# Chunk 2's first product in half-size products, keys-values and last numerators in one burst, and a preparation spread over two chunks

## The chip, the cores and the metric

The kernel runs on one core of a Trainium2 chip. The metric is the device time of one execution in microseconds, the median of three runs. One further execution was profiled; all rows quoted here come from it.

## The reference

Two steps follow each other: a linear attention with cosine weights, and a two-layer MLP with a swish whose slope is learned per hidden unit.

```
B, H, S, D = 8, 8, 576, 64
q_p, k_p = [relu(x)*cos_w, relu(x)*sin_w]          # 2*D features per head
kv  = einsum('bhsf,bhsd->bhfd', k_p, v)             # keys-values
z   = sum(k_p, axis=2)
num = einsum('bhsf,bhfd->bhsd', q_p, kv)            # numerators
den = einsum('bhsf,bhf->bhs', q_p, z) + 1e-6
x   = (num/den), laid out as [4608 tokens, 512]
h   = x @ w_in                                      # 512 -> 2048
g   = h / (1 + exp(-beta*h))
out = g @ w_out                                     # 2048 -> 512
```

## The kernel before

The attention is worked on batch by batch (8 batches of 576 tokens, or nine blocks of 64), the MLP chunk by chunk (nine chunks of 512 tokens, or eight blocks). Chunk c needs the last blocks of batch c-1 and the first ones of batch c. While chunk c goes through the MLP, the attention of batch c+1 and the preparation of later batches run beside it. All matmul operands are bf16, sums are in PSUM, which has eight banks (`ps`).

A batch passes through these steps. Its q, k and v are loaded on SP's queue (`load_raw`, one buffer each). `q_relu` writes `qb`; a transposing DMA on SP's queue (`q_turn_dma`, TQ) turns it into `qts`, of which there are two, one for even and one for odd batches; `q_tan` multiplies that by a tangent into the second half of the query features (`qs_of`), on GpSimd (POOL in the profile) or VectorE (DVE). `k_relu` writes `rk`. `v_scale` writes `vb`, the values times the cosine and times the sine, in nine steps each. `kv_mm` (L276) makes the keys-values from `rk` and `vb` with 72 matmuls of 64x64 tiles in two PSUM banks; `kv_take` (L286) copies them to `kv`. `num_mm` (L297) makes the numerators with 64x64 tiles, `num_all` a third of a batch (three of nine token groups, both head pairs, 48 matmuls). `x_part` divides (L308, L312, L319) into `xs` and turns it with a transposing DMA into the chunk's `xt` (L367).

A chunk's MLP has two halves, named h and o here. In full size, h is 16 groups of four 128x512 matmuls (`h_mm`, L386), each followed by the swish on ScalarE (ACT; `h_act`, L394). In half-size products (the scheme of Strassen and Winograd), a pair of groups takes seven products of halves instead of eight, each two matmuls of 256 columns (`h_pair`, L511), and sums before and after them: sums of weights (`wh_sum`, L443, once for all chunks), sums of x (`x_sum`, L455, four per chunk), and in PSUM a copy to a second bank on ACT (`seed`, L480), a copy to SBUF (`keep`, L484) and two additions on DVE (`add`, L487) per pair; the swish is `h_silu` (L420). The second product, o, is in half-size products from chunk 1 on: 2 x 7 products of eight matmuls with 256 columns (`o_fast`, L562, in chunk 1; `o_pair`, L620, from chunk 2 on), with sums of g on DVE (`g_sum`, L406, 16 per chunk). Chunks 0 to 2 make h in full size, chunks 3 to 8 in half size.

The scheduling is manual: every engine and every queue carries out its instructions in the order in which the program issues them, and waits where data or a buffer is not ready. Up to chunk 2's h the order is written as Python (the slots, `h_first`). From then on it is written out in `ORDERS`, one string of steps per chunk, which `chunk` issues from left to right:

- `h35` is product 5 of pair 3 of h; `1` and `c` name a PSUM bank behind them (`h110`, `h1c6`). `ox`, `oy` are o's two halves. `c` is the seed, `d`/`D` the keep on ACT/DVE, `e` and `f` the additions, `A`, `B` the swish of h, or the copies of o out of PSUM on ACT (`X`, `Y` on DVE).
- `s21` is g_sum of kind 2 for the second four groups of g, `W51` the weight sum of kind 1 for pair 5, `t1` an x_sum of the next chunk.
- `K00` and `K1` are keys-values for the two head pairs (bank 0 and the next), `kT` the copy to `kv`; `N12` numerators of third 1 in bank 2 and the next, `x1` their division and turn.
- `k`, `v`, `w`, `q`, `g`, `TQ`, `L` prepare and load later batches: k_relu on ACT, values times sine on ACT, times cosine on DVE, q_relu on DVE, tan on POOL, the turn of q, the loads.

Where `g` is issued, `q_tan` makes POOL wait for the DVE step that `chunk` remembers as `last`:

```
    def q_tan(b, jp, behind=None):
        got = tan_mul(nc.gpsimd, qs_of(b)[:, jp], qts[b % 2][:, jp], 0, NQ)
        after(got, behind, "GpSimd behind a copy")
```

Stores of o are issued on POOL's queue up to chunk 6 (`store`, L536).

Of the kernel before, what the change touches and what calls it, by code (L numbers as in the profile page):

```python
# [16 lines left out]
P = 128  # L17
# [5 lines left out]
def kernel(  # L23
# [175 lines left out]
    def k_relu(b, j0=0, j1=4, eng="dve", n0=0, n1=NQ):  # L199
        relu(rk.rearrange("q n j d -> q j n d")[:, j0:j1, n0:n1], raw_tile(b, "k")[:, j0:j1, n0:n1], eng)  # L200
# [48 lines left out]
    def qs_of(b):  # L249
        return wx["q"] if b > 3 and b % 2 == 0 else qs_first  # L250
# [15 lines left out]

    def kv_out(jp, bank):
        return ps[:, bank : bank + 2, jp * 2 * E : (jp + 1) * 2 * E]
# [12 lines left out]
    def kv_take(jps, bank, eng="dve"):  # L281
        a0, a1 = jps[0], jps[-1] + 1
        o = kv[:, :, a0:a1].rearrange("q g s c e -> q g (s c e)")
        a = ps[:, bank : bank + 2, a0 * 2 * E : a1 * 2 * E]
        if eng == "act":
            nc.scalar.copy(o, a)  # L286
        else:
            nc.vector.tensor_copy(o, a)

    def num_mm(b, n, jp, bank, slot):  # L290

        for cs in range(2):
            for jj in range(2):
                rows = slice(jj * HP, (jj + 1) * HP)
                for g in range(2):
                    cols = slice(g * HP, (g + 1) * HP)
                    nc.tensor.matmul(  # L297
                        ps[cols, bank + jj, slot * E : (slot + 1) * E],
                        lhsT=(qts[b % 2], qs_of(b))[cs][rows, jp, n, cols],
                        rhs=kv[rows, g, jp, cs, :],  # L300
                        start=(cs == 0), stop=(cs == 1))

    def x_rden(bank, slot, n0, n1, jps):

        w, m = len(jps), n1 - n0
        nv = ps[:, bank : bank + 2, slot * E : (slot + w * m) * E].rearrange("q j (i s e) -> q j i s e", s=w, e=E)
# [25 lines left out]
    def num_all(b, t, bank):  # L332
        for i in range(3):
            for jp in range(2):
                num_mm(b, 3 * t + i, jp, bank, 2 * i + jp)
# [37 lines left out]
    def h_bank(c, jt):  # L373
        if c < 2 and jt < 4:
            return ((3, 2, 5, 0), (6, 7, 4, 5))[c][jt]
        if c == 2 and jt in (10, 11):
            return jt - 8
        return ((6, 7, 4, 5) if c == 0 else (0, 1, 4, 5))[jt % 4]
# [43 lines left out]
    def wx_tiles():  # L422
# [8 lines left out]
            BF16)[:, 0 : 2 * NQ * P].rearrange("q (s n c) -> q s n c", s=2, n=NQ)  # L431
# [123 lines left out]
    def o_fast(c, pr, banks):  # L555

        b_ps, e_ps, a_ps = (ps[:, k_, 0:HM] for k_ in banks)
        tok = slice(pr * P, (pr + 1) * P)

        def prod(dst, left, right, start, stop):  # L560
            for i in range(JT // 2):
                nc.tensor.matmul(dst, lhsT=left(i), rhs=right[:, i], start=start and i == 0,  # L562
                                 stop=stop and i == JT // 2 - 1, skip_group_check=True)

        def g_part(r, hf):
            def at(i):
                jt = 2 * i + r
                return gs[c, jt // 4][:, jt % 4, hf * (TCH // 2) + pr * P : hf * (TCH // 2) + (pr + 1) * P]
            return at

        def s_part(t):
            return lambda i: t[:, i, tok]

        o1 = osb_pool.tile([P, DM], FP32, name="o_sb", tag="o_sb")
        o2 = osb_pool.tile([P, DM], FP32, name="o_sb", tag="o_sb")
        p1 = part.tile([P, HM], FP32, name="p1", tag="p1")
        p5 = part.tile([P, HM], FP32, name="p5", tag="p5")
        u = part.tile([P, HM], FP32, name="u", tag="u")

        def c4():  # L580
            nc.scalar.copy(o2[:, 0:HM], b_ps)

        def stored(key, op):
            def do():
                op()
                waits[key[0]].discard(key[1:])
                if not waits[key[0]]:
                    store(c, pr + (2 if key[0] == "2" else 0), o2 if key[0] == "2" else o1)
            return do

        waits = {"1": {"a2", "a3"}, "2": {"a7", "c4"}}
        add = dict(op=ALU.add)
        return {
            "1": lambda: prod(b_ps, g_part(0, 0), B11, True, False),
            "5": lambda: prod(e_ps, s_part(S1), T1, True, False),
            "6": lambda: prod(b_ps, s_part(S2), T2, False, False),
            "2": lambda: prod(a_ps, g_part(1, 0), B21, True, True),
            "7": lambda: prod(b_ps, s_part(S3), T3, False, False),
            "3": lambda: prod(e_ps, s_part(S4), B22, False, True),
            "4": lambda: prod(b_ps, g_part(1, 1), T4, False, True),  # L600
            "c1": lambda: nc.scalar.copy(p1, b_ps),
            "c5": lambda: nc.scalar.copy(p5, e_ps),
            "cu": lambda: nc.scalar.copy(u, b_ps),
            "c4": stored("2c4", c4),
            "a2": stored("1a2", lambda: nc.vector.tensor_tensor(o1[:, 0:HM], a_ps, p1, **add)),
            "a3": stored("1a3", lambda: nc.vector.tensor_tensor(o1[:, HM:DM], e_ps, u, **add)),
            "a7": stored("2a7", lambda: nc.vector.tensor_tensor(o2[:, HM:DM], b_ps, p5, **add)),
        }


# [107 lines left out]
    kv_take((0,), 6, eng="act")  # L718
# [14 lines left out]
    kv_take((1,), 6, eng="act")  # L733
# [56 lines left out]
    def second():  # L790
# [18 lines left out]
        22: lambda: (kv_mm(1, 0, 6), kv_mm(1, 1, 6), kv_take((0, 1), 6, "act"), q_relu(1, 1, "act", 5)),  # L809
# [34 lines left out]
    def kv_all(b, bank=6, eng="dve"):  # L844
        kv_mm(b, 0, bank)
        kv_mm(b, 1, bank)
        kv_take((0, 1), bank, eng)
# [33 lines left out]
    for slot in range(16):  # L881
# [10 lines left out]
        elif slot == 6:  # L892
            w_sums()
        elif slot == 10:
            kv_all(2, eng="act")
            for jp in range(2):
                tan_mul(nc.vector, qs_of(2)[:, jp], qts[0][:, jp], 0, NQ)
    q_relu(3, 0, "act")
    q_relu(3, 1, "act")
    q_turn_dma(3)  # L900

    def one_sums(kind):
        for i0 in range(0, JT // 2, 2):
            g_sum(1, i0, i0 + 2, kind)

    def ops(of, names):
        for n in names.split():
            of[n]()

    x, y = o_fast(1, 0, (2, 5, 4)), o_fast(1, 1, (3, 7, 6))  # L910
    ops(x, "1 c1")
    one_sums(1)
    ops(y, "1 c1")
    for t, bank in enumerate((4, 6, 0)):
        num_all(2, t, bank)
    one_sums(2)
    x_part(2, 0, 4)
    ops(x, "6 cu")
    ops(y, "6 cu")
    one_sums(3)  # L920
    ops(x, "2 5 c5")
    x_part(2, 1, 6)
    ops(x, "7")
    one_sums(4)
    ops(x, "a2 a7")
    ops(y, "7 2")
    got = wh_sums(0)
    x_part(2, 2, 0)
    load_raw(4, "q")
    q_tan(3, 0, got)  # L930
    q_tan(3, 1)
    ops(y, "a2 5 c5")
    ops(x, "3 a3 4 c4")
    ops(y, "a7 3 a3 4 c4")
    v_half(3, 0)

    ORDERS = {
        2: (
            "ox16 W61 N12 N00 oy17 x0 oxc4 oyc5 ox5 ox6 oxd k2 k0 k3 k1 v5 x1 N20 oxe W62 oy6 v4 v1 v3 oy5 Lk x2 oyD "
            "oye v0 ox7 q1 q0 w2 w8 ox3 ox2 oy3 w1 w3 oy7 w7 oy2 v7 w5 w6 oyf w4 oxf oy4 v8 W64 ox4 oyX W63 v6 oyB w0 "  # L940
            "t1 t3 t2 v2 oxA t4 Lv Lq oxB"),
        3: (
            "W51 h012 TQ h213 K00 h2c5 W11 h0c7 K1 h22 kT h05 h25 h06 h26 h0d h02 h2d W31 h110 h15 h311 h1c4 h0e h35 "
            "h2e W12 h07 W13 h0f W32 h27 h03 h1d h3d h2f h3c6 h23 h0A W52 h2A h12 W14 h04 W71 h36 W33 W72 h24 h16 h517 "
            "h1e W34 h0B h32 h3e h615 h2B h55 h13 h712 h75 h5D h37 h1A h33 h5c3 h3f h17 h3A h7D h65 h52 h1f h7c4 h6D "
            "g0 h34 h56 h5e h416 W54 W73 h3B h14 h6c1 h76 h72 h1B h45 h53 h4c0 W53 h4d h62 W74 h57 h66 h7e h73 h5A h6e "
            "h5f h77 g1 h42 h7A v7 h46 h7f h4e h67 h63 h54 h6f w2 h74 h6A h47 h43 h4A N03 h64 h5B oy11 h7B h4f h6B h44 "
            "ox10 h4B s11 s30 w4 x0 w6 s10 oyc7 N13 N25 s13 oxc2 s12 s20 v6 v8 k0 ox5 oxd s22 k3 ox2 oy5 w5 v1 s21 k1 "
            "s23 s32 ox6 v2 v3 x1 s31 oxe oyd s42 s40 s41 oy2 oy6 s43 w8 w3 ox3 s33 oye ox7 oy3 q1 v4 v0 w1 w7 k2 Lk "
            "w0 oy7 oxf v5 oyf ox4 t1 oy4 x2 oxB Lv oyY oxA q0 Lq t2 oyA t4 t3"),  # L950
        4: (
            "h113 h014 h05 h215 h15 K06 h0c0 h2c2 h1d TQ h1c1 K1 h0D kT g1 h16 h12 h26 h1e h25 h22 h06 h2d h0e h13 h2e "
            "h316 h17 h35 h07 h1A h3d h23 h3c1 h03 h0f h1f h02 h27 h2A h36 h04 h0A h0B h617 h65 h14 h3e h2f h37 h512 "
            "h1B h410 h24 h3f h4c4 h55 h34 s10 h713 h45 h46 h6D h2B h3B h33 h5D h4D h5c5 h32 h42 h6c6 s30 h75 h56 h3A "
# [136 lines left out]
```

## Time and profile before

| | |
|---|---|
| three runs | 274.15, 274.15, 274.41 us; median 274.15 |
| the profiled execution | 274.55 us, span 272.8 us |
| TensorE (PE) busy | 265.6 us, 97% of the span |
| PE weight loads | 207.0 us, 76% |
| VectorE (DVE) busy | 224.3 us, 82% |
| ScalarE (ACT) busy | 188.6 us, 69% |
| GpSimd (POOL) busy | 67.5 us, 25% |
| chunk 1, h and o | 51.9 to 66.25, then to 80.15 us |
| chunk 2, h and o | to 95.2, then to 109.05 us |
| chunk 3, h and o | to 122.6, then to 136.6 us |
| end of the last matmul | about 268.4 us |

The times are counted from the span's start. Busy time is the time in which at least one instruction of the engine is open. An instruction's length holds its latency, so that two that follow each other overlap in the record: the pitch of a run of equal ones is shorter than the mean of one. Rows of a window give the length, then per engine the busy time and the instructions in it. Rows of a timeline give start, length, engine, line, operation, tiles, shapes and how many were merged.

### The profile page before, as it was taken

The page shows a single profiled execution, that of the slowest core. Times are in us where ns is not written, and L with a number is a line of the kernel's source. Part 1 is how long each engine was busy: PE and PEld are TensorE (multiplying, and loading weights), DVE is VectorE, ACT ScalarE, POOL GpSimd, SP SyncE. Part 2 cuts the span into 40 slices and gives each one's busy share as a digit, 9 for nine tenths or more (in the row PEclk, how much of TensorE's full clock was granted, in tenths as well). Part 3 has the DMA queues.
Part 4 walks back from the last instruction along what each step waited for, and adds up shares of the span by engine and source line. Part 5 has one row for each costly group of instructions (what it writes and reads, how often), then busy time and mean ns, then how long its engine had stood idle before and what let it go on. Part 6 is the DMA issues. An engine that isn't in the chain of part 4 may idle for free.

```text
span 272.8 us, 8972 instructions
## 1 busy us (share of the span) xinstructions
PE 265.6 (97%) x3712; PEld 207.0 (76%) x3712; DVE 224.3 (82%) x596; ACT 188.6 (69%) x384; POOL 67.5 (25%) x87
## 2 busy tenths in 40 slices
PE   8889999999999999999999999999999999999993
PEld 8554455445874488888888888888888888888882
DVE  5889959499999989789989996999599768748841
ACT  4778777797329656899489967996695179329910
POOL 1454000510078000560094009300930060000000
PEclk9999999999999999999999999999999999999999
DMA  7999999999959999893689339944500460024006
GB/s 221 388 390 377 394 390 312 394 207 344 278 114 331 215 362 258 264 296 67 190 210 353 85 63 244 293 70 83 162 1 8 77 163 2 2 47 110 0 6 151
DMA packets 50745, 54.00 MB, mean 198 GB/s; under 512 B 31232, under 2 KB 31760, under 8 KB 50704
## 3 DMA queue, kind: packets, MB, share of 16 engines
q1 hardware_dynamic: 47664, 45.82, 59.1%
q0 software_dynamic: 2688, 7.34, 9.2%
q8 instruction: 29, 0.48, 0.7%
q10 hardware_dynamic: 352, 0.27, 0.4%
q14 instruction: 12, 0.10, 0.1%
HBM read 36.71 MB, written 9.44 MB: 169 GB/s over the span
## 4 chain that ended last, share of the span: by engine, by line
PE 91%; DMA 3%; DVE 2%; SPq 1%; issue 1%
PE ps L620 32%; PE ps L511 27%; PE ps L386 15%; PE ps L543 5%; PE ps L562 5%; PE ps L297 4%; DMA raw_v<-in_v_dram 3%; PE ps L276 3%; DVE xs L319 1%; SPq L79 1%; PE ps L356 0%; PE ps L235 0%; DVE win L115 0%; DVE rden L312 0%; DVE vb L209 0%
## 5 line engine op out<-in xcount | busy, mean ns | idle before, releaser
L420 ACT ACTIVATE g_t<-ps,beta 128x512 bf16<-128x512 f32 x96 | 60.4, 704 | 1.4 <-PE ps L511 1.3
L536 POOL DMA_DIRECT2D out_dram<-o_sb x56 | 32.9, 594 | 103.7 <-ACT o_sb L657 44.0
L620 PEld LDWEIGHTS <-S 128*128 128x128 bf16 x448 | 43.4, 98 | 5.2
L511 PE MATMUL ps<-w_stage 128*128 128x256 bf16 x288 | 46.6, 272 | 0.1
L386 PE MATMUL ps<-xt,win 128*128 128x512 bf16 (+1 forms) x196 | 42.8, 375 | 0.1
L511 PEld LDWEIGHTS <-w_stage 128*128 128x128 bf16 x384 | 37.3, 98 | 5.1 <-issue 0.3
L487 DVE TENSOR_TENSOR ps<-ps,p 128x256 f32<-128x256 f32 x74 | 30.5, 427 | 8.6 <-PE ps L511 3.0
L394 ACT ACTIVATE g_t<-ps,beta 128x512 bf16<-128x512 f32 x48 | 32.3, 689 | 7.2 <-PE ps L386 7.1
L620 PEld LDWEIGHTS <-g_t 128*128 128x128 bf16 x336 | 32.3, 98 | 4.5 <-ACT g_t L420 0.4
L386 PEld LDWEIGHTS <-win 128*128 128x128 bf16 x196 | 18.8, 98 | 21.0 <-issue 0.4
L511 PE MATMUL ps<-xt,win 128*128 128x256 bf16 x192 | 32.9, 273 | 0.0
L511 PEld LDWEIGHTS <-win 128*128 128x128 bf16 x288 | 28.0, 98 | 3.5
L620 PE MATMUL ps<-wout,g_t 128*128 128x256 bf16 x224 | 28.9, 273 | 0.0
L406 DVE TENSOR_TENSOR S<-g_t 128x512 bf16<-128x512 bf16 (+1 forms) x66 | 25.7, 418 | 2.6 <-ACT g_t L420 1.7
L480 ACT COPY ps<-ps 128x256 f32<-128x256 f32 x62 | 22.6, 384 | 7.5 <-PE ps L620 4.0
L217 ACT ACTIVATE vb<-raw_v,sin 128x256 bf16<-128x256 f32 (+1 forms) x58 | 26.0, 505 | 2.5 <-DMA raw_v<-in_v_dram 2.5
L620 PE MATMUL ps<-T,S 128*128 128x256 bf16 x224 | 26.6, 273 | 0.0
L620 PE MATMUL ps<-wout,S 128*128 128x256 bf16 x224 | 26.4, 273 | 0.0
L319 DVE TENSOR_TENSOR xs<-ps,rden 128x768 bf16<-128x768 f32 (+4 forms) x26 | 22.8, 883 | 0.9 <-DVE rden L312 0.2
L223 POOL TENSOR_TENSOR qs<-qt,tanr 128x1152 bf16<-128x1152 bf16 x6 | 14.3, 2391 | 27.4 <-PE ps L562 21.0
L219 DVE TENSOR_SCALAR vb<-raw_v,cos 128x256 bf16<-128x256 f32 x63 | 20.3, 371 | 0.0
L657 ACT COPY o_sb<-ps 128x512 f32<-128x512 f32 x11 | 6.3, 587 | 20.1 <-PE ps L620 20.1
(112 smaller groups left out, 410.7 us busy)
## 6 DMA issues: line engine op xcount, KB each, us to landing
raw_v<-in_v_dram SPq DMA_DIRECT2D x7, 1152.0 KB, 9.7
raw_k<-in_k_dram SPq DMA_DIRECT2D x7, 1152.0 KB, 9.4
raw_q<-in_q_dram SPq DMA_DIRECT2D x7, 1152.0 KB, 7.4
out_dram<-o_sb POOLq DMA_DIRECT2D x56, 128.0 KB, 4.7
w_stage<-in_moe_w_in_dram SPq DMA_DIRECT2D x3, 1024.0 KB, 13.2
w_stage<-in_moe_w_out_dram SPq DMA_DIRECT2D x2, 1024.0 KB, 8.0
w_stage<-in_moe_w_out_dram SPq DMA_DIRECT2D x4, 512.0 KB, 11.9
out_dram<-o_sb SPq DMA_DIRECT2D x12, 128.0 KB, 2.4
```

The source lines that it names most:

```text
L217: got = nc.scalar.activation(o, a, AF.Copy, scale=t[:, n : n + 1])
L219: got = nc.vector.tensor_scalar(o, a, scalar1=t[:, n : n + 1], scalar2=None, op0=ALU.mult)
L319: nc.vector.tensor_tensor(o.rearrange("q j n s d -> q j (n s) d"), nv[:, :, a:z, :, 0:D].rearrange("q j n s d -> q j (n s) d"), rden[:, :, ...
L386: nc.tensor.matmul(ps[:, h_bank(c, jt), i * 64 : (i + w) * 64], lhsT=win[jt // 4][:, mi, (jt % 4) * P : (jt % 4 + 1) * P], rhs=xt[:, i : i ...
L394: return nc.scalar.activation(gs[c, jt // 4][:, jt % 4], ps[:, h_bank(c, jt)], AF.Silu, scale=beta[:, jt : jt + 1])
L406: return nc.vector.tensor_tensor(o, l, r, op=op)
L420: return nc.scalar.activation(gs[c, jt // 4][:, jt % 4], bank, AF.Silu, scale=beta[:, jt : jt + 1])
L480: return nc.scalar.copy(at("a", 0), at("b", 0))
L487: nc.vector.tensor_tensor(dst, at("b", 0), st["p5"], op=ALU.add)
L511: nc.tensor.matmul(dst, lhsT=l[:, g], rhs=r[:, :, g * HP : (g + 1) * HP], start=start and g == 0, stop=g == 1, skip_group_check=True)
L536: (eng or own).dma_start(out=out_v[bb, n][:, m0:m1], in_=o_sb[hf * HP : (hf + 1) * HP, m0:m1])
L620: nc.tensor.matmul(dst, lhsT=l(i), rhs=r[:, i], start=start and i == 0, stop=i == order[-1], skip_group_check=True)
```

## The change

- Chunk 2's h goes in half-size products (`h_pair`), and so all weight sums are made earlier, in chunks 1 and 2. `h_first` is gone, and chunk 2 is issued from `ORDERS` as a whole.
- Chunk 1's o goes through `o_pair` and `ORDERS` instead of `o_fast`, which is gone. Of batch 2, the keys-values and the tan move from chunk 1's h into this order; one of its two tans goes to POOL (`g1`), the other stays on DVE (`G0`).
- The keys-values of batch c+1 move from the head of chunk c's h to its end, and are followed by the last third of the numerators of batch c (`N2`), which move there from chunk c-1's o. The first two thirds of batch c+1 are issued by `M0`, `M2`, `M1`, `M3`, each a third for one head pair (24 matmuls). `kv` has a second buffer for that (`kv_of`), and its copy is issued by head pair (`ka`, `kb` on DVE, `kA`, `kB` on ACT).
- The two PSUM banks of K, N and M need no longer be neighbours (`two`): K036 uses banks 3 and 6.
- The steps that prepare a batch are counted for each kind (`after_last`) and may lie in two chunks. Each has a form on the other engine: `V` sine on DVE, `z` cosine on ACT, `j` k_relu on DVE, `y` q_relu on ACT.
- The turn of q (TQ) of batch c+2 stands behind N2 in chunk c, in chunk 1 behind x1 and in chunk 5 near its end. The orders of all chunks are new. `fill` and `filled` have no effect with these orders.

```diff
-        return wx["q"] if b > 3 and b % 2 == 0 else qs_first
+        return wx["q"] if b > 1 and b % 2 == 0 else qs_first
...
+    def kv_of(b):
+        return wx["kv"] if b > 1 and b % 2 == 0 else kv
+
+    def two(bank):
+        if isinstance(bank, int):
+            return ps[:, bank : bank + 2]
+        return ps[:, bank[0] : bank[1] + 1 : bank[1] - bank[0]]
...
-    def num_all(b, t, bank):
+    def num_all(b, t, bank, jps=(0, 1), fill=False):
         for i in range(3):
-            for jp in range(2):
-                num_mm(b, 3 * t + i, jp, bank, 2 * i + jp)
+            for jp in jps:
+                num_mm(b, 3 * t + i, jp, bank, 2 * i + jp, not fill or i == jp == 0)
...
-        if c == 2 and jt in (10, 11):
-            return jt - 8
...
-    def o_fast(c, pr, banks):
...
         elif slot == 6:
             w_sums()
-        elif slot == 10:
-            kv_all(2, eng="act")
-            for jp in range(2):
-                tan_mul(nc.vector, qs_of(2)[:, jp], qts[0][:, jp], 0, NQ)
-    q_relu(3, 0, "act")
-    q_relu(3, 1, "act")
-    q_turn_dma(3)
...
-    x, y = o_fast(1, 0, (2, 5, 4)), o_fast(1, 1, (3, 7, 6))
...
     ORDERS = {
+        1: (
+            "y1 g1 oy12 s11 s30 s21 K036 kA s13 K1 ox17 G0 kB oyc0 s32 M014 s12 oxc5 M2 M136 s10 M3 ox2 y0 x0 x1 k0 k3 "
+            "TQ W71 oy2 oy5 ox5 s20 k2 s22 s23 s41 s33 k1 W63 oxd ox6 oy6 oyd v1 oxe z8 s31 W11 ox7 W51 v7 oye s42 s40 "
+            "v4 s43 z5 oy7 W01 W52 W31 z2 W72 oyf W21 W02 oy3 z0 z7 W32 W12 V8 oxf ox3 v6 W61 oyA oy4 W13 ox4 z4 oxA "
+            "W33 z3 z1 v0 W22 oyB t1 t3 t2 W74 oxB t4"),
         2: (
-            "ox16 W61 N12 N00 oy17 x0 oxc4 oyc5 ox5 ox6 oxd k2 k0 k3 k1 v5 x1 N20 oxe W62 oy6 v4 v1 v3 oy5 Lk x2 oyD "
...
+            "h011 h114 h313 W34 W54 h35 h15 h1c0 h216 h0c5 h25 h3c2 W24 h36 h1d W14 h3d h2c7 h05 h16 h3e h1e h0D Lq "
+            "h32 h2d h26 h33 h2e h37 W23 h12 h17 W41 h13 h23 h22 h1f v2 V5 v3 h06 z6 h3A W04 W42 h1A h0e h27 h2A h14 "
+            "h1B h412 h3f h510 W53 h5c7 h45 h02 h2f W44 h34 h4c4 h03 W62 h24 h3B h55 W03 W64 Lk h4D q1 h42 h52 h46 h56 "
+            "h613 h0A h07 h2B h65 h4e h43 h6c5 W43 h716 y0 h62 h0f h04 h5D h6D h66 h5e h47 h75 h53 h57 h6e h0B h67 "
+            "h7c1 h63 h76 h72 g0 h4f h7d h5A h4A h5f h6f h54 h7e h64 h5B h6B W73 Lv s11 Lq s30 h44 h73 h77 h6A s21 "
+            "K047 s10 K1 N203 s20 h7f h74 h7A k2 h7B oy15 h4B v8 z0 ox11 kb g1 k1 TQ z3 ka oxc6 x2 s13 V2 s41 oyc2 s12 "
+            "s23 M003 s31 M2 M147 s22 M3 oy5 s43 ox5 ox6 v5 s33 s32 oxd w1 oy2 v1 oyd x0 v4 k3 oy6 s40 oxe x1 ox2 ox7 "
+            "z4 s42 v6 v7 v3 ox3 y1 j0 oye w6 V0 oy7 oxX oy3 oyf y0 z8 oxf oy4 ox4 oyX z7 oxY t1 t2 t3 oyB t4 Lk"),
         3: (
-            "W51 h012 TQ h213 K00 h2c5 W11 h0c7 K1 h22 kT h05 h25 h06 h26 h0d h02 h2d W31 h110 h15 h311 h1c4 h0e h35 "
...
+            "s32 K015 h7f Lq s10 h5B s21 h6f K1 N227 kB h63 h74 h64 h6A ox16 Lv ka TQ j0 h7B oy10 s12 x2 M027 s22 h6B "
...
         7: (
-            "h111 h212 h25 h315 h1c7 h2c3 h016 h15 h3c0 h16 h26 h1D h12 h05 h2d h22 h36 h1e h2e h0c4 h0d h35 h32 h13 "
...
+            "h113 N206 h012 h1c5 h15 h1d h214 h25 x2 h16 h0c1 h12 h05 h06 h1e h2c7 h26 h02 h13 h0D h2d h310 h0e h17 "
...
+    same = {"V": "v", "z": "w", "j": "k", "y": "q"}
+    seen = {"Lq": 3, "Lk": 3, "Lv": 3}
+
+    def after_last(op):
+        op = same.get(op[0], op[0]) + op[1]
+        seen[op] = seen.get(op, 2) + 1
+        return seen[op]
...
-            elif k_ == "N":
-                parts[n] = bank
-                num_all(b, n, bank)
+            elif op in ("ka", "kb", "kA", "kB"):
+                kv_take(b, ("ab".index(op[1].lower()),), parts["k"], "act" if op[1] in "AB" else "dve")
+            elif k_ in "Nn":
+                parts[2] = bank
+                num_all(c, 2, bank, fill=k_ == "n")
+            elif k_ in "Mm":
+                if n < 2:
+                    parts[n] = bank
+                num_all(b, n % 2, parts[n % 2], (n // 2,), n % 2 in filled)
...
+            elif k_ == "G":
+                last = tan_mul(nc.vector, qs_of(b)[:, n], qts[b % 2][:, n], 0, NQ)
...
-    h_first(2)
     held = None
-    for c in range(2, NTC):
+    for c in range(1, NTC):
         held = chunk(c, held)
```

## The prediction

> **What bounds the kernel now.** I read, in order: the page's busy times, the windows by stage, TensorE's timeline, then the timelines of the engines that feed it. In the windows of chunk 1's o, chunk 2's h, chunk 2's o and chunk 7's h (columns: length; busy time and instructions of PE, weight loads, DVE, ACT, POOL; clock; DMA):
>
> ```profile
> 66.20:80.10 13.90, 13.87 (x258) 12.25 (x256) 13.12 (x37) 5.19 (x10) 3.41 (x2) 1.00 0.93 232
> 80.10:95.20 15.10, 15.10 (x139) 7.28 (x137) 14.82 (x41) 11.98 (x21) 7.84 (x9) 1.00 1.07 263
> 95.20:109.10 13.90, 13.90 (x259) 12.18 (x257) 12.30 (x37) 8.24 (x19) 0.50 (x1) 1.00 1.07 304
> 219.20:231.20 12.00, 12.00 (x112) 10.75 (x110) 9.64 (x27) 10.65 (x24) 3.40 (x7) 1.00 0.32 89
> ```
>
> PE is busy throughout at full clock, so a matmul less is time less. But in these first three DVE works 40.2 of 42.9 us, and chunk 2's h is where the change adds DVE work. Next, PE's timeline: one full-size run, one half-size run, and a numerator burst with its neighbours.
>
> ```profile
> 63.71 2.54 PE L386 MATMUL ps<-xt,win 128*128 128x512 bf16 x11
> 97.81 1.91 PE L620 MATMUL ps<-T,S 128*128 128x256 bf16 x16
> ...
> 121.73 0.38 PE L511 MATMUL ps<-xt,w_stage 128*128 128x256 bf16 x2
> 122.05 0.22 PE L297 MATMUL ps<-kv,qt 64*64 64x65 bf16 x4
> ...
> 122.42 0.20 PE L297 MATMUL ps<-kv,w_stage 64*64 64x65 bf16 x4
> 122.56 0.39 PE L511 MATMUL ps<-w_stage,win 128*128 128x256 bf16 x2
> ```
>
> Pitch is (run less last matmul's length) over the rest: (2.54-0.379)/10 = 0.216 us for 512 columns, (1.91-0.273)/15 = 0.109 for 256. The burst: the two L511 end their pitch at 121.95, it starts at 122.05; its 48 matmuls at 8.3 ns fill to 122.45, the next L511 starts at 122.56. So each change of tile size costs 0.1 us, a burst 0.2.
>
> **PE's part.** Chunk 2's h: 64 matmuls x 0.216 = 13.8 go (trace: 80.15 to 95.21, less 1.15 for a keys-values burst, 13.9); 8 pairs x 7 products x 2 = 112 x 0.109 = 12.2 come. -1.6 us. Weight loads grow from 64 to 112, hidden as in chunk 7 (10.75 of 12.0).
> Bursts: before, chunk 1 has 2 (K; all N), chunks 2 to 6 three each (K; two N; one N): 17. After: chunk 1 has 2, chunks 2 to 6 two each (K with N2; four M), chunk 7 one: 13. Four fewer x 0.2 = -0.8. The matmuls inside are the same, and o_pair in chunk 1 issues the 112 products of o_fast.
> K leaves the head of h. There ACT's 0.59 us copy of kv waited for K; at chunk 4 PE then stood 0.24 and 0.44 us behind a DVE add. Between 0 and -0.7; I take -0.4, the one stall that occurs.
> Together -2.8, all on the path.
>
> **DVE and ACT.** Costs are pitches from runs (last length taken off): DVE adds and 128x512 sums 0.335, W sums 0.20, v 0.265, x 1.33 (0.20+0.26+0.87), two-input tan 1.27; ACT silu 0.58, 256-column copy 0.27, v 0.40, k 0.57, q half 1.06. Half-size h adds to chunk 2 on DVE 16 adds, 4 copies (6.7 us), four x sums (1.3) and 16 more W sums (3.2); moved to ACT or later: most v (3.5), k (1.3). Summed over the new orders, DVE has 15.6 in chunk 1's o, 26.4 in chunk 2: 42.0, of which s11, s30, s21 (1.0) can run before h ends. PE has 14.4 (112 x 0.109, K 0.95, four M 0.8, bursts 0.4) and 27.0 (the same with 224 and N2's 0.4): 41.4. So DVE is level with PE. In order, DVE comes from s13 at 65.9 to the end of t1 in 13.4, at 79.3; h35 wants it at 65.1+14.4+0.65 = 80.1. From chunk 3 on DVE has 22 to 24 per chunk against 27: slack.
> ACT in chunk 2's h: 8+4 copies, 15 silus, three v, a q half, a k, 14.9 in PE's 13.8. Up to h6B, whose bank N2 needs, ACT's sum ends near 13.3 and PE wants it at 13.1; oy1's last matmul wants h7A at 14.5 and gets it near 14.6. Bounds 0 (chunk 8's h ran with ACT at 11.8 of 12.0 and no stall) and 1.2 (all of ACT's excess over PE); I take +0.4, the two small gaps with a handover each.
>
> **The first tan of batch 2, and GpSimd's hold on DVE.** The change takes two DVE tans out of chunk 1's h and gives one (g1) to POOL with nothing to wait behind (held is None). Before shows what a POOL tan does to DVE (timelines of both):
>
> ```profile
> 59.42 1.22 DVE L875 TENSOR_TENSOR T<-wout 128x2048 bf16<-128x2048 bf16 x1
> 63.08 1.22 DVE L878 TENSOR_TENSOR wout<-wout 128x2048 bf16<-128x2048 bf16 x1
> 76.69 4.73 POOL L223 TENSOR_TENSOR qs<-qt,tanr 128x1152 bf16<-128x1152 bf16 x2 [20.97 <-PE ps L562]
> 79.65 4.01 DVE L219 TENSOR_SCALAR vb<-raw_v,cos 128x256 bf16<-128x256 f32 x9
> 146.12 2.39 POOL L223 TENSOR_TENSOR qs<-qt,tanr 128x1152 bf16<-128x1152 bf16 x1 [2.58 <-DVE S L406]
> 148.17 0.62 DVE L406 TENSOR_TENSOR S<-g_t 128x512 bf16<-128x512 bf16 x1
> ```
>
> Nine v took 4.01 us where nine at 54.48 took 2.45: the 1.6 more is the tan's rest to 81.42. The S sum took 0.62 for 0.42 and ended 0.28 after the tan. DVE adds that read PSUM kept 0.43 under the same tan.
> g1 can start when qt of batch 2 lands: issued at 55.57, shortest landing 6.2, so 61.8, to 64.2, over the third and fourth weight sum. They end at 66.7 instead of 64.3. Then s11, s30, s21 to 67.7, s13 68.0, G0 69.3. PE, whose h now ends at 66.25-1.15 = 65.1, wants G0's result for M0 after oy1, K, ox1: 65.1+0.87+1.15+0.87 = 68.0. PE waits 1.2 us. Without the hold s13 waits only for the last silu (65.9) and G0 ends at 67.5: no wait. Bounds 0 and 1.7 (the whole lag); I take +1.2, since DVE's ops there are the kind that waited. Behind M0 in PE's queue stand the other M and all of o. The same lag would reach ox6, whose S2 sums come 0.7 to 1.1 late; a PE that has stood 1.2 at M0 finds them ready.
> The Trainium skill (SBUF — State Buffer, section on two separate sides) has the pair of ports as an exclusive lock for whoever starts first, against a DVE instruction with two SBUF inputs: a DVE sum could then hold off g1 as well. No run here shows POOL waiting (all ten tans took 2.38 to 2.40); if it did, g1 and the sums would still add up to 69.3 for G0, and my term stays.
> The later g0 and g1 are tied behind a DVE step and followed by DVE work that reads PSUM, so I cost them at nothing; where that cover fails, one costs DVE up to its 2.4.
>
> **SP and POOL queues.** TQ moves from the head of h to behind N2, which still reads the qt that it overwrites, and stands right ahead of the turns of x2, x0, x1, on which the next h waits. Its time on SP:
>
> ```profile
> 69.10 4.27 SPq L259 DMA_TRANSPOSE qt<-qb  x1
> 110.36 11.72 SPq L259 DMA_TRANSPOSE qt<-qb  x1
> ```
>
> 4.3 alone, 11.7 behind two loads issued just before. The new loads wait only for the preparation of the batch before, and SP runs ahead of the written order: in chunks 3 and 4 they are out 8 us before TQ. In chunk 2 the second Lq goes out about 10 us into the chunk, TQ at 13.5. Taking 7 there, x2, x0, x1 (four turns x 1.25, landing 1.5 later) are in at 27.0, as DVE comes to t1. So 0; the other end is among the rivals. POOL's stores stay at the ends of o. The copies of kv (ka, kb; 0.36 each) lie under oy1 and ox1, 1.74 long; without that cover PE waits up to 0.7. N2's x2 is due a chunk later, in chunk 7 by t1 in mid-h.
>
> **Sum.** -1.6-0.8-0.4+1.2+0.4 = -1.2. The profiled execution, 274.55 (span 272.8 and 1.75 around it), becomes 273.35; it lies 0.4 above the median of 274.15, which becomes 273.0.
>
> **Rivals.**
> DVE bound in chunks 1 and 2 (slower). DVE's sum of 41.0 leaves no room for waits. Before, it idled 0.54, 0.70, 0.30 and 0.31 between 79 and 107, and 2.0 in chunk 3's half-size h. If those 3.9 and the hold's 1.7 add up, DVE ends chunk 2 at 65.9+41.0+5.6 = 112.5; the next h tolerates some 2.1 of that (its t4 came at 138.66 with PE at 136.57), so PE is at 110.4 against 65.1+41.4 = 106.5. 3.9 of stall for the 1.6 of my sum: 275.3. It decides from 2.8 us of stall. Against it: chunk 2's h held 98% DVE without a stall, though PE did not wait on it step by step.
> TQ too long (slower). If chunk 2's TQ takes 11.7, the turns are in at 13.5+11.7+5.0+1.5 = 31.7 and t1 at 32.1, where h35 wants it at 27.7: 4.4 late, 277.4. For: three of six TQ took over 10. Against: each of those had 2.3 MB issued in the 2 us before.
> Work falls, but the stalls take it (no change): 2.2 to 3.3 of stall in all, as when the hold costs 1.7 and ACT 1.2: 274.3.
> No hold (faster still): the 1.2 falls away, 271.8. For it: no tan has yet lain over a 2048-wide sum of this kind. Against: the waits of the v and S rows above.
> That the products don't get cheaper is excluded by chunk 7: the same 112 took 12.0.
>
> **How the numbers follow.** A run of this kernel can be told from no change beyond about 0.2%, 0.55 us. My forecast has 0.45 and no hold 0.15, both faster. Stalls take it: 0.15. DVE bound: 0.15. TQ: 0.10. Faster 0.60, same 0.15, slower 0.25. Low end 271.4: no hold, K's full 0.7. High end 275.4: the DVE rival. Outside lie TQ's 0.10 and another 0.10 for what goes past the two ends. The range of the likeliest case alone is 271.4 to 273.6.
>
> **What would show it.** Chunk 2's h: 112 L511 at 0.109 and no L386 after 66. Thirteen bursts, K and N2 touching. A gap on PE of about 1.2 us near 68 with GpSimd's tan over the L877 sum. L420 near 96% of ACT in chunk 2's h, with gaps under 0.5 before N2. Wrong if PE stands for more than 2.8 us between 66 and 110, or if TQ of batch 4 takes over 8 us.

## The result, and the profile after

The changed kernel takes 333.88 us (median of four runs, 333.53 to 335.5) where the kernel before took 274.28 beside it: 1.218 times as long, 95% interval 1.214 to 1.222. The prediction was 273.0, with a range up to 275.4. It is wrong by 61 us, and in sign.

The profiled execution has a span of 331.8 us. The page's busy times, and the windows that answer to those of before (chunk 1's o, chunk 2's h, chunk 2's o, chunk 7's h):

```profile
PE 281.0 (85%) x3756; PEld 215.6 (65%) x3760; DVE 234.6 (71%) x613; ACT 198.3 (60%) x405; POOL 67.8 (20%) x88
```

```profile
65.36:83.53 18.17, 15.22 (x281) 12.61 (x280) 16.02 (x46) 12.18 (x27) 1.15 (x2) 1.00 0.91 247
83.53:100.12 16.59, 14.95 (x234) 12.41 (x232) 14.36 (x47) 15.48 (x36) 6.50 (x10) 1.00 0.84 298
100.12:122.94 22.82, 16.30 (x210) 13.37 (x208) 13.04 (x33) 11.80 (x25) 3.54 (x5) 0.85 0.37 81
269.91:285.96 16.05, 13.74 (x161) 11.01 (x159) 9.98 (x26) 12.10 (x26) 2.63 (x6) 1.00 0.46 85
```

No engine is the bound: TensorE (PE) falls from 97% to 85%, and DVE and ACT, with some 10 us more work each, fall to 71% and 60%. The engines stand for each other. The loss is in every chunk, in chunk 8 too, which has no keys-values, no numerators and no preparation. Lengths in us, each from the first matmul of one stage in TensorE's timeline to that of the next, in chunk 8 to the end of the last matmul (the last two columns are experiments below):

| | before | after | n_order | n_plan2 |
|---|---|---|---|---|
| chunk 1, o | 13.9 | 18.2 | 18.5 | 16.0 |
| chunk 2 | 28.9 | 39.4 | 32.0 | 29.0 |
| chunk 3 | 27.5 | 34.4 | 31.7 | 28.0 |
| chunk 4 | 27.4 | 41.0 | 31.7 | 28.5 |
| chunk 5 | 27.8 | 39.5 | 31.4 | 28.4 |
| chunk 6 | 27.4 | 32.1 | 29.2 | 29.0 |
| chunk 7 | 24.6 | 28.6 | 27.0 | 26.0 |
| chunk 8 | 24.7 | 28.6 | 28.7 | 25.0 |

Four rows of the waits, each with who waited, for whom, and the total, the number and the longest of these waits in us:

```profile
PE ps L305 <- DVE xs L327: 11.7, 6, 3.7
DVE den L316 <- PE ps L581: 8.7, 3, 3.9
PE ps L581 <- DVE xs L327: 8.1, 5, 2.5
ACT ps L497 <- DVE xs L327: 5.7, 4, 2.1
```

L327 is `x_mul`, the division of the numerators, L305 the numerators, L316 the first step of `x_part`, L581 o's products, L497 the seed. A product of o has no business with a division: they share neither data nor a bank. One such knot, at the start of chunk 2's o, on DVE, on ACT and on TensorE:

```profile
101.67 0.76 DVE L296 CAST kv<-ps 128x260 bf16<-128x260 f32 x2 [1.86 <-ACT g_t L435]
104.28 0.17 DVE L316 TENSOR_TENSOR den<-ps,eps 128x12 f32<-128x12 f32 x1 [1.84 <-ACT ps L497]
104.75 0.96 DVE L327 TENSOR_TENSOR xs<-ps,rden 128x768 bf16<-128x768 f32 x1
```

```profile
103.82 0.43 ACT L497 COPY ps<-ps 128x256 f32<-128x256 f32 x1
105.80 0.36 ACT L497 COPY ps<-ps 128x256 f32<-128x256 f32 x1 [1.55 <-DVE xs L327]
```

```profile
100.12 1.91 PE L581 MATMUL ps<-wout,g_t 128*128 128x256 bf16 x16
105.76 0.27 PE L305 MATMUL ps<-kv,qt 64*64 64x65 bf16 x4 [3.73 <-DVE xs L327]
107.24 4.90 PE L581 MATMUL ps<-T,S 128*128 128x256 bf16 x24
```

The order there is `N203 ... ox11 kb ... ka oxc6 x2 ... oyc2 ... M003`. `x2` reads banks 0 and 3 through the view `ps[:, 0:4:3]`. Its first step waited 1.84 for `oxc6`, a seed that reads bank 1 and writes bank 6; then `oyc2`, which writes bank 2 from bank 5, waited 1.55 for `x2`. Banks 1 and 2 lie between 0 and 3. `kb` (banks 4 and 7) stood for a silu in the same way. M0 needs bank 0 and really had to wait for `x2`, so TensorE stood 3.73 for all of it.

In the built program each wait leads to the instruction that ends it, and each instruction to its banks. The changed kernel has 74 waits in which the two have no bank in common and one uses two distant banks; the kernel before has none.

The lowered clock came on top. Windows of 4 us around that knot:

```profile
104.00:108.00 4.00, 2.24 (x100) 1.97 (x100) 3.65 (x11) 1.04 (x3) 0.00 (x0) 0.60 0.27 54
108.00:112.00 4.00, 4.00 (x23) 2.82 (x22) 1.25 (x4) 0.00 (x0) 0.00 (x0) 0.55 0.01 1
112.00:116.00 4.00, 2.05 (x18) 1.54 (x16) 2.61 (x8) 3.82 (x10) 0.00 (x0) 1.00 0.05 11
```

In the two windows from that stand on the granted clock was 0.60 and 0.55, and 24 matmuls took 4.90 (the row at 107.24) where 24 at full clock take 2.78. It fell in the same way at the stands that end at 189.74 and 222.26 us. Over the whole span it was 0.972; before it was 1.00.

### The profile page after: what moved, and what is told of

Same layout as the page of the kernel before. It is cut to its first block, busy times and chain, and to the rows that moved or that the text cites. A ratio compares the mean times of both kernels' runs of the same rounds, so it can differ in the third digit from the quotient of the medians.

```text
span 331.8 us, 9138 instructions
## 1 busy us (share of the span) xinstructions
PE 281.0 (85%) x3756; PEld 215.6 (65%) x3760; DVE 234.6 (71%) x613; ACT 198.3 (60%) x405; POOL 67.8 (20%) x88
## 5 line engine op out<-in xcount | busy, mean ns | idle before, releaser
L581 PEld LDWEIGHTS <-S 128*128 128x128 bf16 x512 | 51.9, 103 | 21.8 <-issue 8.8
L528 PE MATMUL ps<-w_stage 128*128 128x256 bf16 x336 | 55.2, 272 | 8.1 <-ACT ps L497 4.7
L528 PEld LDWEIGHTS <-w_stage 128*128 128x128 bf16 x448 | 43.3, 97 | 21.3 <-issue 13.5
L581 PEld LDWEIGHTS <-g_t 128*128 128x128 bf16 x384 | 37.7, 99 | 10.0 <-issue 4.9
L528 PE MATMUL ps<-xt,win 128*128 128x256 bf16 x224 | 38.2, 272 | 2.4 <-DVE ps L504 2.1
L528 PEld LDWEIGHTS <-win 128*128 128x128 bf16 x336 | 32.5, 97 | 10.1 <-issue 5.6
L581 PE MATMUL ps<-T,S 128*128 128x256 bf16 x256 | 34.7, 293 | 4.9 <-DVE xs L327 2.2
L497 ACT COPY ps<-ps 128x256 f32<-128x256 f32 x72 | 24.8, 368 | 21.5 <-PE ps L528 8.0
L581 PE MATMUL ps<-wout,S 128*128 128x256 bf16 x256 | 32.2, 281 | 5.9 <-DVE xs L327 3.4
L581 PE MATMUL ps<-wout,g_t 128*128 128x256 bf16 x256 | 32.6, 276 | 4.6 <-DVE xs L327 2.5
L401 PE MATMUL ps<-xt,win 128*128 128x512 bf16 (+1 forms) x132 | 28.5, 373 | 0.1
L504 DVE TENSOR_TENSOR ps<-ps,u 128x256 f32<-128x256 f32 x43 | 18.4, 428 | 10.2 <-PE ps L528 4.0
L421 DVE TENSOR_TENSOR S<-g_t 128x512 bf16<-128x512 bf16 x64 | 24.7, 416 | 0.9 <-ACT g_t L435 0.9
L327 DVE TENSOR_TENSOR xs<-ps,rden 128x768 bf16<-128x768 f32 (+4 forms) x26 | 22.8, 883 | 0.8
L501 DVE COPY p<-ps 128x256 f32<-128x256 f32 x28 | 11.7, 422 | 16.0 <-PE ps L528 7.5
L305 PEld LDWEIGHTS <-qt 64*64 64x64 bf16 x576 | 12.0, 113 | 16.5 <-issue 15.6
L528 PE MATMUL ps<-xt,w_stage 128*128 128x256 bf16 x112 | 20.7, 272 | 1.6 <-DVE ps L504 1.4
## 6 DMA issues: line engine op xcount, KB each, us to landing
w_stage<-in_moe_w_out_dram SPq DMA_DIRECT2D x4, 512.0 KB, 11.9
```

What stands on the lines that cost most here:

```text
L305: nc.tensor.matmul(two(bank)[cols, jj, slot * E : (slot + 1) * E], lhsT=(qts[b % 2], qs_of(b))[cs][rows, jp, n, cols], rhs=kv_of(b)[rows, ...
L327: nc.vector.tensor_tensor(o.rearrange("q j n s d -> q j (n s) d"), nv[:, :, a:z, :, 0:D].rearrange("q j n s d -> q j (n s) d"), rden[:, :, ...
L401: nc.tensor.matmul(ps[:, h_bank(c, jt), i * 64 : (i + w) * 64], lhsT=win[jt // 4][:, mi, (jt % 4) * P : (jt % 4 + 1) * P], rhs=xt[:, i : i ...
L421: return nc.vector.tensor_tensor(o, l, r, op=op)
L497: return nc.scalar.copy(at("a", 0), at("b", 0))
L501: return (nc.scalar.copy if eng == "act" else nc.vector.tensor_copy)(st["p5"], at("b", 1))
```

## Experiments

All times are medians; ratios are to the kernel before, run beside them, with 95% intervals.

| run | us | ratio |
|---|---|---|
| changed kernel | 333.88 | 1.218 (1.214 to 1.222) |
| e1_near | 301.45 | 1.098 (1.096 to 1.100) |
| b_far | 292.45 | 1.065 (1.061 to 1.069) |
| e8_tail | 297.51 | 1.085 (1.081 to 1.088) |
| e_ka | 300.24 | 1.094 (1.092 to 1.095) |
| n_order | 301.28 | 1.100 (1.098 to 1.102) |
| n_flip | 293.44 | 1.070 (1.068 to 1.072) |
| n_flip_g | 292.55 | 1.066 (1.064 to 1.068) |
| n_plan | 303.91 | 1.109 (1.107 to 1.111) |
| f_plan | 315.40 | 1.150 (1.147 to 1.154) |
| n_plan2 | 281.48 | 1.026 (1.023 to 1.029) |
| n_plan3 | 285.59 | 1.039 (1.035 to 1.044) |
| n_plan4 | 287.56 | 1.049 (1.046 to 1.052) |

### Distant banks: e1_near, b_far

In the changed kernel, only digits change (chunk 1 shown); in the kernel before, digits and the view:

```diff
# e1_near
-            "y1 g1 oy12 s11 s30 s21 K036 kA s13 K1 ox17 G0 kB oyc0 s32 M014 s12 oxc5 M2 M136 s10 M3 ...
+            "y1 g1 oy12 s11 s30 s21 K067 kA s13 K1 ox13 G0 kB oyc0 s32 M045 s12 oxc1 M2 M167 s10 M3 ...
# b_far
-        nv = ps[:, bank : bank + 2, slot * E : (slot + w * m) * E].rearrange(...)
+        nv = two(bank)[:, :, slot * E : (slot + w * m) * E].rearrange(...)
...
-            "W51 h012 TQ h213 K00 h2c5 W11 h0c7 K1 h22 kT ...
+            "W51 h012 TQ h211 K003 h2c4 W11 h0c5 K1 h22 kT ...
```

> The changed kernel with its PSUM banks renumbered chunk by chunk, so that the two banks of every K, N and M lie next to each other again; steps, order and work are the same, and no instruction spans banks that it doesn't use. Theory A (the new pair view of two distant banks makes instructions wait for work in the banks between them): the program then has none of the 74 waits between instructions without a common bank, the TensorE gaps behind L327 (23.9 us) and most of those behind the DVE additions go, the granted clock stays at 1.00, and the time falls from 333.9 to between 273 and 285. Theory B (the new orders overload VectorE or hold the same-bank work of two engines back): the gaps stay, 320 to 334.

> The kernel before with its banks renumbered in chunks 3 to 6, so that the two banks of every K and N lie three to seven apart and are reached through the changed kernel's pair view; order and work are the same. The program then has 56 waits between instructions without a common bank where it had none. Theory A: about 56/74 of the changed kernel's loss at most, so 280 to 320 instead of 274.3, with TensorE gaps behind the division (L324 here). Theory B: 274.3, within 0.6.

In both, and so in e8_tail and e_ka, which start from e1_near, the renumbering lets a bank that numerators filled only in part become the second bank of a pair at a chunk's start. Some sums of h come out changed there, with the same instructions in the same places: their times can be compared, their outputs are not the kernel's.

e1_near: 301.45, so 32.4 us go with the 74 waits; TensorE's waits for L327 fall from 21.4 us (11.7 and 8.1 above, and 1.6; the expectation had 23.9) to 0.5, and the clock is 1.00. b_far: 18.0 us more than the kernel before, with gaps of the changed kernel's kind (TensorE's timeline; the waits):

```profile
126.55 0.22 PE L302 MATMUL ps<-kv,qt 64*64 64x65 bf16 x4 [1.22 <-DVE xs L324]
```

```profile
PE ps L625 <- DVE xs L324: 7.8, 7, 1.6
```

That settles the view as a cause, from both sides. It falls short of my expectation: 27 us of loss are left in e1_near, which theory A had at 285 at most. n_order repeats e1_near with another renumbering that leaves all sums as they were:

> The changed kernel with the two banks of every pair next to each other, by another renumbering than e1_near: here each partly written bank of one chunk is taken first by a product 1 in the next, as in the changed kernel itself. Same steps, same order. Both theories: as e1_near, 301.4 within 1. It is the base of the next two.

301.28. It is the base of what follows.

### Chunk 8's order, and kA: e8_tail, e_ka

```diff
# e8_tail: e1_near with chunk 8 in the order of before: the same 147 steps, four keeps on the other engine
-            "h311 h217 h015 h116 h05 h0D h15 h2c2 h0c0 h1D h35 h25 h06 h26 h1c3 h12 h3c4 ...
+            "h217 h011 h05 h315 h2c6 h112 h26 h25 h0c0 h3c3 h2D h06 h35 h32 h02 h15 h36 h2e ...
```

> As the renumbered kernel, with chunk 8 in the order of the kernel before. Chunk 8 has no K, N, M or division; in the changed kernel it took 28 us where it took 24.6 before. Theory C (its new order costs time by itself, the keep on VectorE standing ahead of the seed on ScalarE at the same bank): 2 to 3.5 us less than the renumbered kernel. Theory A alone: chunk 8 only inherited a late start, the same time within 0.6.

> As the renumbered kernel, with chunk 1's first copy of the keys-values (kA) issued behind K1 instead of between K0 and K1. In the changed kernel K1 stood 1.76 us behind that copy, which reads the same two banks, and G0 (the tan behind GpSimd's hold on VectorE) ended at 69.6 while the M0 that needs it started at 70.4. Theory D (the copy holds K1, and hides the hold's cost): K1 follows K0 without a gap, about 1 us less than the renumbered kernel, and M0 waits for G0 instead. Theory E (the copy's wait costs nothing of its own, the end is set by VectorE in chunk 1's o): the same within 0.3.

e8_tail is 3.9 us under e1_near, a little past the expected 2 to 3.5, and its chunk 8 takes 24.7, as in the kernel before: one chunk's order, with the same steps but for the engine of four keeps, costs 4 us by itself. e_ka is 1.2 under e1_near in the median. K1 follows K0 without a gap, and what my prediction had comes out from behind it (e_ka: TensorE, DVE):

```profile
69.39 0.23 PE L305 MATMUL ps<-w_stage 64*64 64x65 bf16 x4 [1.03 <-DVE w_stage L223]
```

```profile
63.32 3.41 DVE L839 TENSOR_TENSOR wout<-wout 128x2048 bf16<-128x2048 bf16 x1
68.00 1.34 DVE L223 TENSOR_TENSOR w_stage<-qt,tanr 128x1152 bf16<-128x1152 bf16 x1
```

The last weight sum takes 3.41 for 1.22 under GpSimd's tan, and TensorE waits 1.03 at M0 for G0. So in the profiled executions chunk 1's o is only 0.45 shorter (17.80 to 17.35). Another 0.7 lies in chunk 6, whose order is the same in both, and is not the copy's.

### The same queues, another interleaving: n_flip, n_flip_g

Why does an order cost 4 us in a chunk that lacks nothing? Two steps of different engines on one bank also wait for each other when they use its two halves. In the built n_order there are 177 waits between two instructions that share a bank but no address, one of them writing, and 52 where both only read; the kernel before has 100 and 51. Which of the two waits depends on which is issued first. n_flip has every engine's and every queue's own sequence as in n_order, instruction for instruction and bank for bank, and only issues them in another interleaving (found by search, with each sequence held fixed). In chunk 2's o, for instance:

```diff
-  ox17 kb g1 k1 TQ z3 ka oxc0 x2 s13 V2 s41 oyc3 s12 s23 M056 s31 M2 M112 s22 M3 oy5 ...
+  x2 s13 M056 M2 M112 M3 V2 z3 s41 s12 oy5 oxc0 oyc3 ...
```

> As n_order; every engine and every queue carries out the same instructions in the same order with the same banks. Only the interleaving in which the program issues them is another, and with it which of two instructions on different engines that touch one bank waits for the other. Theory G (what is left of the loss are waits between two engines for one bank, mostly for its other half, whose direction the new order has against the flow): 10 to 16 us less than n_order. Rival F (what is left is work: VectorE or ScalarE overloaded, GpSimd's hold, transfers): the queues being the same, no change within 1.

293.44: 7.8 us less than n_order, short of the 10 to 16 expected and far outside the rival's 1. Since no engine does anything else or in another sequence, this part is waits alone. The place above, in n_order (TensorE, ACT):

```profile
104.24 2.78 PE L581 MATMUL ps<-T,S 128*128 128x256 bf16 x24 [1.59 <-ACT ps L497]
```

```profile
102.13 0.56 ACT L217 ACTIVATE vb<-raw_v,cos 128x256 bf16<-128x256 f32 x1
102.52 0.73 ACT L192 ACTIVATE rk<-raw_k 128x576 bf16<-128x576 f32 x1
103.09 0.55 ACT L217 ACTIVATE vb<-raw_v,cos 128x256 bf16<-128x256 f32 x1
103.50 0.70 ACT L497 COPY ps<-ps 128x256 f32<-128x256 f32 x2
```

and in n_flip:

```profile
100.64 2.79 PE L581 MATMUL ps<-T,S 128*128 128x256 bf16 x24
```

```profile
101.00 0.37 ACT L497 COPY ps<-ps 128x256 f32<-128x256 f32 x1
101.78 0.36 ACT L497 COPY ps<-ps 128x256 f32<-128x256 f32 x1 [0.41 <-PE ps L581]
```

`oy5` writes the second half of a bank whose first half the seed `oyc3` copies. Issued behind the seed, it waits 1.59 us for a copy that stands on ACT behind preparation; issued ahead, it goes at once and the seed waits 0.41. The number of such waits is the same in both programs (177); their direction is what counts. Each stand of TensorE after 55 us can be matched to the wait of the built program that ends it. Waits for a step that shares a bank but no address end 12.3 of 19.8 us of stands in n_order, 4.0 of 12.5 in n_flip, 0.1 of 22.5 in n_plan and 1.0 of 5.1 in n_plan2 (the last two are below).

The Trainium skill (PSUM — Partial Sum Buffer, section on bank collisions) states that two engines must not be in one bank and the same 32 partitions at once, whatever addresses they use, two readers included, and that semaphores should guard a bank and not an address. So these waits can't simply be dropped. No run here lets two engines in at once; the runs show only what keeping them apart costs.

n_flip_g puts GpSimd's tan onto DVE:

```diff
-            "y1 oy12 K067 g1 K1 ox13 kA kB s11 s30 s21 s13 oyc5 G0 M001 ...
+            "y1 oy12 K067 K1 ox13 kA kB s11 s30 s21 s13 oyc5 G0 G1 M001 ...
```

> As n_flip, with the second tan of batch 2 on VectorE right behind the first (G0 G1) instead of on GpSimd (g1). In n_flip the tan on GpSimd ran from 63.24 and two S sums that take 0.74 together took 2.95; G0 ended at 69.2, and TensorE stood 1.03 at M0 for it, at 69.3. My prediction's term (GpSimd's hold delays G0, TensorE waits some 1.2): the sums are 2.2 earlier, the gap at M0 goes, 0.7 to 1.1 less than n_flip. Rival (VectorE is full in chunk 1's o, 1.27 more on it comes back later): same within 0.3, or slower.

292.55, 0.9 less in the median, within the 0.7 to 1.1 expected; the two intervals barely part. The two sums take 0.75 again, and the gap at M0 is gone. But the profiled execution, which took 294.56, does not show the gain at its place: chunk 1's o takes 17.1 us in it and 17.0 in n_flip. TensorE comes to the next steps earlier and stands there for something that the profile does not name (n_flip_g; in n_flip this stand is 0.34):

```profile
72.38 1.59 PE L581 MATMUL ps<-T,S 128*128 128x256 bf16 x13 [1.09 <-issue]
```

So how much of the 0.9 the hold accounts for stays open. This execution also lost 2.0 us in chunk 6, where the granted clock was 0.57 from 216 to 220 us, around a stand of 2.23; n_flip's stand of 2.00 there left it at full clock.

### Other orders of the same steps: n_plan, f_plan, n_plan2, n_plan3, n_plan4

These hold n_order's steps, banks, engines and chunks and reorder each chunk, by a search that lets one engine at a time into a bank. f_plan is n_plan with the changed kernel's digits. A piece of chunk 1:

```diff
-            "y1 g1 oy12 s11 s30 s21 K067 kA s13 K1 ox13 G0 kB oyc5 s32 M001 s12 oxc4 M2 M167 s10 M3 ...
+            "K067 K1 s13 s12 y1 g1 ox13 v0 W33 s11 z5 oy12 s10 kA oy5 G0 ox5 s32 kB M001 M167 ...
```

> As n_order with the same steps and banks, but the steps of each chunk put in another order, made so that the one-bank rule holds nothing up; no step is taken out, added or moved to another engine or chunk. Theory G: all 27 us of n_order's loss go, and what my prediction summed for the work itself remains: 270 to 275, TensorE 97% busy. Rival F: work that does not fit cannot be ordered away, over 285.

> As n_plan with the changed kernel's own bank numbers, the pairs two to six banks apart. 63 waits between instructions without a common bank come back. Theory A: 15 to 32 us more than n_plan, as between the changed kernel and n_order (32.4), since the order now is as little made for them as that one was. Rival: with an order that fits, they fall into slack, under 5 us.

n_plan takes 303.91, more than n_order. By its number that is rival F's forecast. The trace gives another reason: the bank stalls were gone, but waits for transfers and for steps put too late had come (ACT's timeline, TensorE's):

```profile
72.72 0.52 ACT L217 ACTIVATE vb<-raw_v,sin 128x256 bf16<-128x256 f32 x1 [5.79 <-DMA raw_v<-in_v_dram]
```

```profile
120.81 0.60 PE L528 MATMUL ps<-xt,win 128*128 128x256 bf16 x4 [3.06 <-DMA xt<-xs]
```

The search had taken loads and turns as shorter than they are, so a step that needs a load had moved ahead of kA. f_plan is 11.5 us above n_plan: distant banks cost here too, less than the 15 to 32 I expected and more than the rival's 5.

> As n_order, the same steps and banks, in another order than n_plan. n_plan lost its time at other places than n_order: 2.7 us behind values that came 5.8 us after ScalarE was ready for them, 3.1 and 2.9 behind turns of x that landed late, 1.6 behind sums that GpSimd's tan held. This order leaves the loads, the turns and the tan the time that those rows show. Theory G (work and transfers fit, only the order kept them from it): 268 to 276, below the kernel before if my sum for the work was right (-1.2, or -2.4 without the hold). Rival F (work that doesn't fit): over 285.

> A second order of the same kind, from another start. Theory G: 268 to 278. Rival F: over 285. If the two differ by over 3 us, what remains hangs on single places and not on the amount of work.

n_plan2 gives the loads, turns and tans the lengths of those rows: 281.48. So 19.8 of n_order's 27.0 us go by order alone, and rival F is out as the main cause: the same work fits into 281.5. It missed theory G's range by 5 us. n_plan3, of the same kind, takes 285.59: past theory G's range, and by the number alone just in rival F's. The two differ by 4.1, more than the 3 named, so single places count: n_plan3's longest stand is 2.11 at 73.39, again one that the profile does not name. GpSimd's hold is visible in what is left of n_plan2 (DVE, POOL, TensorE):

```profile
199.37 2.46 DVE L219 TENSOR_SCALAR vb<-raw_v,sin 128x256 bf16<-128x256 f32 x1
```

```profile
196.95 4.72 POOL L223 TENSOR_TENSOR qs<-qt,tanr 128x1152 bf16<-128x1152 bf16 x2 [0.18 <-DMA qt<-qb]
```

```profile
202.21 0.38 PE L528 MATMUL ps<-w_stage,win 128*128 128x256 bf16 x2 [1.37 <-DVE ps L504]
```

A v, which takes 0.34 to 0.37 a few us before, takes 2.46 beside the second of the two tans (199.3 to 201.7); the add that follows is late, and TensorE stands 1.37.

> As n_plan2, the same steps and banks in a third order, made with 0.27 us kept free at each handover between two engines, since n_plan2 still lost 7 us in small waits of that size (TensorE's longest gap there 1.37). Theory G: under n_plan2's 281.5, at 274 to 280; below 274.3 if the work fits as my sum had it. Rival F in its small form (some 7 us of work on VectorE and ScalarE don't fit whatever the order): 281 to 284.

287.56: worse than n_plan2 and outside both forecasts. Keeping room at each handover did not help. Its premise was off: of the 5.1 us that TensorE stands after 55 us in n_plan2, two stands are 2.6 (1.37 above, and 1.19 at 71.95). In n_plan4 TensorE stood 2.3 before numerators at 102.0, and the clock fell to 0.91 in the 20 us after 100. No order tried beats the kernel before. Whether one exists for this change is open.

## Why the prediction was wrong

**The step that failed: what the new orders and the pair view do to waits.** The prediction summed each engine's work, and took waits from data, from a bank that the next step needs and from GpSimd's hold. It had none between two engines on the two halves of a bank, and none for a bank that an instruction does not use. Of `two` it priced nothing, as if that edit only renamed banks. It cost 32.6 us (333.88 less n_order's 301.28, confirmed by b_far's 18.0 in the other direction). Its condition stood in the diff: a step of 3 over a range of 4 spans the two banks between.

**The second part of that step: order.** I summed chunk 2 over the new orders and left chunks 3 to 8 at "From chunk 3 on DVE has 22 to 24 per chunk against 27: slack". A slack in sums says nothing on steps that take turns on one bank. This cost up to 27.0: at least 7.8 is the direction of waits alone (n_flip), 19.8 goes with the best order found (n_plan2), and 7.2 is left in n_plan2. Its stands of 5.1 us on record (before: 0.1) are part of that, 1.37 for GpSimd's hold and 1.19 for no step that the profile names; the rest stays unexplained.

**PE's part.** The pitches hold, but what they were to save is not seen. 112 L528 stand where 64 matmuls were, at a pitch of (1.25-0.27)/9 = 0.109 (after, TensorE):

```profile
122.94 1.25 PE L528 MATMUL ps<-xt,win 128*128 128x256 bf16 x10
```

There are 13 bursts, K and N2 touching. But even in n_plan2 chunk 2's h takes 15.1 us (80.4 to 95.4) with K and N2 in it, as before with K alone. Of my -2.8 there is at most the N2 that it holds besides, some 0.6. By the pitches the products take 12.2 of it, K some 1.15 and N2 some 0.6; about 1.1 is left for handovers and stands (an estimate from these rows). The change turns 64 matmuls that need only ACT behind them into 112 with 32 handovers to DVE and ACT in between, and each is a turn on a bank; the pitch sum left these out. That they must cost is not shown: in chunk 7 of the kernel before, the same 112 took 12.0.

**K off the head of h; the copies at nothing.** The -0.4 assumed that K's stall goes. It moved: chunk 1 issues `K0 kA K1`, the copy reads the banks that K1 writes, and K1 stood 1.76 (after, TensorE). I priced the copies at nothing "under oy1 and ox1", with 0.7 if uncovered; this one lies between K0 and K1, where nothing covers it. e_ka takes the wait away and gains 1.2 in the median, of which the traces show 0.45 in chunk 1's o.

```profile
68.80 0.70 PE L284 MATMUL ps<-vb,rk 64*64 64x130 bf16 x36 [1.76 <-ACT w_stage L294]
70.41 0.22 PE L305 MATMUL ps<-w_stage,qt 64*64 64x65 bf16 x4
```

**The hold (+1.2).** Right in mechanism, and near in the wait it makes, 1.03 (after, POOL and DVE):

```profile
62.59 3.36 POOL L223 TENSOR_TENSOR w_stage<-qt,tanr 128x1152 bf16<-128x1152 bf16 x1 [6.32 <-DVE T L837]
```

```profile
63.63 3.40 DVE L839 TENSOR_TENSOR wout<-wout 128x2048 bf16<-128x2048 bf16 x1
68.30 1.34 DVE L223 TENSOR_TENSOR w_stage<-qt,tanr 128x1152 bf16<-128x1152 bf16 x1
```

G0 ended at 69.64, forecast 69.3. In the changed kernel K1's wait hides it, M0 starting at 70.41; in e_ka and n_flip it shows as 1.03. What it adds to the whole time is not settled, since in n_flip_g another stand takes its place. The prediction knew no run in which GpSimd waits; here it does: its tan took 3.36, 3.45 in n_flip and 3.25 in n_plan2, where the ten before took 2.38 to 2.40. The Trainium skill (SBUF — State Buffer, section on two separate sides) has whichever starts second wait for the whole of the other's instruction. The traces agree: the tan of 62.59 is 1.0 longer, and the sum of 63.63, which starts after it, 2.2.

**ACT (+0.4).** ACT is busy 15.48 of 16.59 us in chunk 2's h, and in n_order TensorE's first gap there is 0.92 for seeds that stand behind v steps: over twice the term, in one place.

**TQ (0).** Right: 3.41 in chunk 1, and 2.85 for batch 4 in chunk 2 (SP):

```profile
75.60 3.41 SPq L259 DMA_TRANSPOSE qt<-qb  x1
100.04 2.85 SPq L259 DMA_TRANSPOSE qt<-qb  x1
```

**The rivals.** DVE as the bound, TQ and no hold are out. "Work falls, but the stalls take it" had the right kind, with 2.2 to 3.3 us of stall from two sources that I had seen. What the text named as proof against itself, PE standing over 2.8 between 66 and 110, is met at 102.0 by one gap, from a source that I had not listed.

## What to carry to other kernels

A PSUM bank is a resource like an engine: count who takes turns on it, halves included, and issue first the step that is ready first, since the one issued second waits whatever its address. Keep the banks that one instruction reaches next to each other; a view with a step is ordered against everything between its ends. And when a new order is in doubt, reissue the same queues in another interleaving: what changes then is waits and nothing else.

## What the runs showed of the hardware

- The granted clock fell at long stands of TensorE: 0.60 and 0.55 in two windows of 4 us from a stand of 3.73 on (changed kernel), 0.82 and 0.76 from one of 3.06 (n_plan, 120 to 128 us), 0.73 and 0.84 from one of 2.11 (n_plan3, 72 to 80 us). The length alone does not decide: 2.53 at 116.83 in the changed kernel left it at 1.00, as did 2.00, n_order's longest. The Trainium skill (TensorE: Matmul & The Clock Gate, section on what's actually happening) has half rate after an idle window of about 3.4 us. The first agrees, and the shorter stands show that such a window need not be idle from end to end.
- GpSimd's hold also takes DVE steps with one SBUF input and a scalar: L219 took 2.46 for 0.35 beside a tan (n_plan2).
- The last of three loads of raw values, 1152 KB each and issued within 1.3 us, was first used 11.9 us after its issue, ACT standing for it (n_plan: v issued at 60.8, its use at 72.7).
- In chunk 1's o TensorE stands for nothing that the profile names: 0.24 to 2.11 us in nine traces with the changed steps, at most 0.03 before. The stand ends 2.46 to 2.57 us after a transfer on the queue that the page calls instruction begins (70.31 and 72.79 in n_flip, 69.81 and 72.38 in n_flip_g, 69.42 and 71.95 in n_plan2). It looks like a wait for the code of the next matmuls; no run tests that.
